# Two transformer layers at decode: all of batch 7's V kept between the layers, a ring of 4 MB for the weights of layer 0, w2 in eight blocks

## The chip, the cores and the metric

The kernel runs on one core of a Trainium2 chip. The metric is the device time of one execution in microseconds (us). A core has engines that run side by side: TensorE (PE in the profile; its weight loads are PEld), VectorE (DVE), ScalarE (ACT), GpSimd (POOL) and SyncE (SP). Here SP does nothing but issue transfers from the chip's main memory. On-chip memory is laid out in 128 partitions.

## The reference

Two equal layers work on eight sequences (batches), one new token each; all is float32, and both layers read the same weights and the same cache.

```
D = 1024; Hq, Hkv, Sk, Dh = 32, 4, 4096, 128; F = 3584; B = 8

def attention(x):                      # x: (8, 1, 1024), x already normed
    q = x @ wq                         # wq 1024 x 4096
    scores = q . k_cache * Dh ** -0.5  # each of 4 K heads serves 8 query heads
    o = softmax(scores) . v_cache
    return o @ wo                      # wo 4096 x 1024

def mlp(x):
    return gelu(x @ w1 + b1) @ w2 + b2 # w1 1024 x 3584, w2 3584 x 1024

for layer in range(2):
    x = x + attention(layernorm(x))
    x = x + mlp(layernorm(x))
```

K and V of one batch are 8.4 MB each, wq and wo 16.8 MB each, w1 and w2 14.7 MB each. The caches are 134 MB for each layer, so the kernel has some 359 MB to read.

## The kernel before

**Memory.** One large tile, `arena`, is cut into 52 units of 1024 columns (`SCW`), 0.52 MB each. Everything that is loaded takes a run of units: a tile of K or V (one of eight for a batch) takes two, and a "piece" of 4 units is 2.1 MB.

**Order of transfers.** A list `stream` is written once, in the order in which the transfers are issued, with the units to which each goes. `pump` issues the first of the list as soon as its units are free, and no other before it. `release` frees units after the last instruction that reads them, and pumps again. All go through SP's queue (the line of `nc.sync.dma_start` in `pump`, L241): an entry whose units are still read by PE holds up all that follow.

**Stages of layer 0.** The queries (`queries`) are made from wq; 28 units of wq (rows `kt` 0 to 6, each in two halves `u`) stay in memory until layer 0 ends, in units 0 to 27, and row 7 is parked elsewhere (`park`, half of it in accumulator memory). The eight batches then run through `attention`: `scores` against K (L545), softmax (`probs`), `values` with V (L588), `heads`. K and V share units 28 to 51. Six of the eight V tiles of the last batch, 7, are not released but stay for layer 1, which runs through the batches from 7 to 0.

**wo, w1.** `project` multiplies with wo (L381), a layernorm follows, and `expand` multiplies with w1 (L270, its last group L273), 512 columns in a group. `hidden_wide` and `hidden_group` turn a group and apply GELU while PE goes on. Both weights pass through units 40 to 51, a ring of 12 units, in pieces of 4 units (two of wo's are 2).

**The swap.** `swap` multiplies with w2 and makes the next layer's queries from the wq that was kept. w2 is cut into four blocks of 256 output columns (`CB`), each with 28 row tiles of 128 (`NFT`). For one block, `down` does 28 products (L418; each float32 product is two matmul records in the profile), DVE copies the sums (L462), PE selects and turns them (L466), DVE adds them to x (L468). With two more rows of x known, PE does the query products of those two rows of wq (`q_part`, L317), and their slots are released. The next parts of w2 and the first K of layer 1 go to those slots. w2, but for its last four row tiles, stays in memory for layer 1; the last four (`LATE`) are read again at the very end.

**Layer 1.** Attention as before, in 28 units; the wo and w1 stages; `down_row` multiplies with the w2 that stayed (L424).

Which part of a block goes to which unit is in this table, by block: (first row tile, number of row tiles, unit).

```
W2_PARTS = (((0, 16, 40), (16, 8, 44), (LAST, 4, 46)), ((0, 4, 47), (4, 16, 48), (20, 4, 46), (LAST, 4, 0)),
            ((LAST, 4, 1), (0, 16, 2), (16, 8, 6)), ((LAST, 4, 0), (0, 16, 8), (16, 8, 12)))
```

Of the kernel before, what the change touches and what calls it, by code (L numbers as in the profile page):

```python
# [38 lines left out]
UNPARK = 14  # L39
# [3 lines left out]
W2_PARTS = (((0, 16, 40), (16, 8, 44), (LAST, 4, 46)), ((0, 4, 47), (4, 16, 48), (20, 4, 46), (LAST, 4, 0)),  # L43
            ((LAST, 4, 1), (0, 16, 2), (16, 8, 6)), ((LAST, 4, 0), (0, 16, 8), (16, 8, 12)))
LATE_AT = 0, 1, 14, 15
# [61 lines left out]
def decode_layers(ctx: ExitStack, tc: tile.TileContext, x, kc, vc, wq, wo, w1, w2, out):  # L107
# [152 lines left out]
    def expand(name, rs, work=None):  # L260
        n = 0
        for slot in tiles((name,)):
            for c in range(0, slot.cols, CH):
                u, kt = divmod(n, NT)
                lhs = xnT[:, kt * XS:kt * XS + 32]
                if kt == 0:
                    acc = ps_o.tile([P, CH], F32, tag="o", name="acc")
                if u < NGR - 1:
                    j = kt % 4
                    nc.tensor.matmul(acc[32 * j:32 * j + 32, :], lhs, slot.ap[:, c:c + CH], start=(kt < 4), stop=(kt >= NT - 4))  # L270
                else:
                    for j in range(4):
                        nc.tensor.matmul(acc[32 * j:32 * j + 32, 0:P], lhs, slot.ap[:, c + j * P:c + (j + 1) * P],  # L273
                                         start=(kt == 0), stop=(kt == NT - 1))
                n += 1
            release(slot)
            if n % NT:
                continue
            if u == 0:
                flush()  # L280
            if u < NGR - 1:
                row = row_s if work or u % 2 else qz[:, P:P + CH]
                nc.scalar.activation(row, acc, AF.Copy, scale=rs)
                if not work:
                    flush()
                pending.append(lambda u=u, row=row: hidden_wide(u, row))
            else:
                if not work:
                    flush()
                row, hid = row_s[:, 0:P], qz[:, P:2 * P]  # L290
                nc.scalar.activation(row, acc[:, 0:P], AF.Copy, scale=rs)
                nc.vector.transpose(hid, row)
                hidden_group(u, lambda pre: nc.vector.tensor_tensor(pre, hid.rearrange("p (t q) -> p t q", t=GT)[:, :, 0:B], bias1(u), ALU.add))
            for f in (work or {}).get(u, ()):
                f()
        assert n == NGR * NT

# [13 lines left out]
    def q_part(acc, u, kt, c0, ap):  # L311

        n = ap.shape[1]
        for j in range(4):
            d0, d1 = max(c0, j * CH), min(c0 + n, (j + 1) * CH)
            if d0 < d1:
                nc.tensor.matmul(acc[u][32 * j:32 * j + 32, d0 - j * CH:d1 - j * CH], xnT[:, kt * XS:kt * XS + 32],  # L317
                                 ap[:, d0 - c0:d1 - c0], start=(kt == 0), stop=(kt == NT - 1 and d1 == (j + 1) * CH))
# [95 lines left out]
    def down(y, c, kts, n0=0):  # L414

        for n, kt in enumerate(kts, n0):
            g = kt % 4
            nc.tensor.matmul(y[32 * g:32 * g + 32], h_at(kt), w2_at[c, kt], start=(n < 4), stop=(n >= NFT - 4))  # L418

    def down_row(y, kts, cs=range(CB)):  # L420

        for kt in kts:
            for c in cs:
                nc.tensor.matmul(y[32 * c:32 * c + 32], h_at(kt), w2_at[c, kt], start=(kt == 0), stop=(kt == NFT - 1))  # L424

    def w2_kts(c, i):

        k0, n, _ = W2_PARTS[c][i]
        return range(k0, k0 + n)

    def arrive(key, kts):
        slot = held[key]
        for e, kt in enumerate(kts):
            w2_at[key[1], kt] = slot.ap[:, e * Q4:(e + 1) * Q4]
        return kts

    def swap():
# [6 lines left out]
        stats = ()  # L444

        def used(kt, u):
            slot = held.pop(("q", kt, u))
            q_part(acc, u, kt, 0, slot.ap)
            release(slot)
            if (kt, u) == (4, 0):  # L450
                st["unparked"] = unpark()

        for c in range(CB):
            y = ys[:, c % 2 * Q4:(c % 2 + 1) * Q4]
            n = 0
            for i in range(len(W2_PARTS[c])):
                kts = arrive(("w2", c, i), w2_kts(c, i))
                down(y, c, kts, n)
                n += len(kts)
            release(held.pop(("w2", c, [k0 for k0, _, _ in W2_PARTS[c]].index(LAST))))  # L460
            ysb = row_s[:, c % 2 * Q4:(c % 2 + 1) * Q4]
# [3 lines left out]
            for i in range(2):  # L465
                nc.tensor.matmul(pt[:, i * B:(i + 1) * B], ysb[:, i * P:(i + 1) * P], bsel, start=True, stop=True)  # L466
            xc = xv[:, 2 * c:2 * c + 2]
            nc.vector.tensor_tensor(xc, pt[:, 0:2 * B].rearrange("p (i b) -> p i b", b=B), xc, ALU.add)  # L468
            if c == CB - 1:
                stats = moments(pt)  # L470
            for kt in (2 * c, 2 * c + 1):
                for u in range(2):
                    if kt < NT - 1:
                        late.append(lambda kt=kt, u=u: used(kt, u))
                        if (kt, u) != (3, 1):
                            late.pop()()
                    elif u == 0:
                        spot = st.pop("unparked")
                        q_part(acc, u, kt, 0, spot.ap)
                        spot.free()  # L480
                    else:
                        slot = held.pop(("qe", 0))
                        q_part(acc, u, kt, 0, slot.ap)
                        q_part(acc, u, kt, W - KEEP, spare)
                        slot.free()
                    if c == CB - 1 and (kt, u) in ((NT - 2, 1), (NT - 1, 0)):
                        next(stats, None)
# [213 lines left out]
    n_kept = 6  # L701
# [24 lines left out]
    for b in orders[0][1:]:  # L726
        batch(0, b, *cycle[(b - 1) % 5])
    weights(("o0",), wo[0], [4, 4, 2, 2, 4, 4, 4, 4, 4], fixed(40, 44, 48, 50, 40, 44, 48, 40, 44))
    weights(("i0",), w1[0], [4] * 7, fixed(48, 40, 44, 48, 40, 44, 48))
    for c in range(CB):  # L730
        for i, (_, _, at) in enumerate(W2_PARTS[c]):
            down_weights(("w2", c, i), c, w2_kts(c, i), at)
    stream.append((("qe", 0), 0, wq[0][:, -W:-KEEP], x_row[:, 0:W - KEEP], ()))
    batch(1, last_b, ((4, 16), (4, 20), (4, 24), (2, 0), (2, 14)), ((4, 16),))
    batch(1, last_b - 1, ((4, 20), (4, 24), (2, 0), (2, 14), (4, 16)), ((8, 28), (8, 16)))
    batch(1, last_b - 2, ((4, 36), (4, 24), (8, 28)), ((8, 16), (8, 24)))
    at = [32, 16, 24] * (4 * B)
    for b in orders[1][3:]:
        batch(1, b, *([(8, at.pop(0)), (8, at.pop(0))] for _ in "kv"))
    weights(("o1",), wo[0], [8, 8, 8, 4, 2, 2], fixed(24, 32, 16, 24, 28, 30))  # L740
    weights(("i1",), w1[0], [4] * 6 + [2, 2], fixed(32, 36, 16, 20, 24, 28, 32, 34))
    for c, e, n in LATE:
        at = (c * NFT + LAST + e) * Q4
# [5 lines left out]
    for layer in range(2):  # L749
# [12 lines left out]
        else:  # L762
# [19 lines left out]
            for c, e, n in LATE:  # L782
                arrive(("late", c, e), range(LAST + e, LAST + e + n))
# [36 lines left out]
def _blocks(w):  # L820
    return w.reshape(NFT, P, CB, Q4).transpose(1, 2, 0, 3).reshape(1, P, -1)
# [38 lines left out]
```

## Time and profile before

| | |
|---|---|
| median of 3 runs | 850.57 us (849.89 to 852.33) |
| the profiled execution | 851.14 us, of which the trace spans 849.4 |
| bytes read | 358.83 MB, 423 GB/s over the span |
| busy | PE 520.2 us (61%), PEld 171.6, DVE 202.2 (24%), ACT 57.0 |
| SP's transfers | 135 issues at L241, all in one queue |
| stages, us from the start | queries to 59; layer 0 attention to 360; wo to 400; w1 to 435; swap to 477; layer 1 attention to 770; wo, w1, w2 to 846 |

A row of a timeline gives the start in us, the duration, the engine, line and operation, what it writes and reads, the shape, how many instructions are taken together, and in brackets how long the engine had been idle and what it waited for. A row of a window gives the stretch and its length, the busy time of PE, PEld, DVE, ACT and POOL with their instruction counts, then the clock that TensorE was granted (1.00 is full), the share of time in which the 16 transfer engines were busy, and GB/s. In the page, DMA and GB/s are given for 40 equal slices of 21.2 us.

### The profile page before, as it was taken

Reading aid. Unit: us, or ns where it says so; the run is one execution under the profiler, and the core shown is the slowest. Engines: PE = TensorE matmul, PEld = TensorE weight load, DVE = VectorE, ACT = ScalarE, POOL = GpSimd, SP = SyncE. Lnnn points to the kernel's source line nnn. Section 1 sums busy time; section 2 is a strip of 40 time slices with the busy share of each in tenths; the row PEclk is TensorE's granted clock in tenths of the full one; section 3 lists DMA queues with packets and bytes.
Section 4 is the critical chain, followed back from the end, with each engine's and each line's share of the span. In section 5 each row is a group of like instructions: output and inputs, shape, how many; then the busy total and the mean of one; then the engine's idle time right before and its main releaser. Section 6 shows DMA issues by size and latency. Waiting matters only on the chain.

```text
span 849.4 us, 9218 instructions
## 1 busy us (share of the span) xinstructions
PE 520.2 (61%) x3962; PEld 171.6 (20%) x3962; DVE 202.2 (24%) x690; ACT 57.0 (7%) x120; POOL 2.2 (0%) x13
## 2 busy tenths in 40 slices
PE   0755755565656647656678775476555566565677
PEld 0211111111111111122133222121111111112333
DVE  0013132222223231400220343231413222231022
ACT  0110000000000000000201100000000000000031
POOL 0000000000000000000000000000000000000000
PEclk9976777786677788877889996868888887869899
DMA  9999999999999999999999999999999999999996
GB/s 401 419 427 436 422 441 419 435 428 432 423 429 441 424 438 418 429 424 427 427 398 416 425 433 426 436 428 433 427 434 428 433 429 432 431 432 430 421 427 273
DMA packets 19768, 359.55 MB, mean 423 GB/s; under 512 B 2192, under 2 KB 2832, under 8 KB 4240
## 3 DMA queue, kind: packets, MB, share of 16 engines
q1 hardware_dynamic: 19584, 358.82, 99.1%
q8 instruction: 31, 0.51, 0.2%
q10 hardware_dynamic: 144, 0.15, 0.1%
q14 instruction: 9, 0.07, 0.0%
HBM read 358.83 MB, written 0.13 MB: 423 GB/s over the span
## 4 chain that ended last, share of the span: by engine, by line
DMA 75%; PE 22%; DVE 1%; issue 1%; another core or an unknown queue 1%; ACT 0%; SPq 0%; ACTq 0%; DVEq 0%
DMA arena<-in_k_dram 29%; DMA arena<-in_v_dram 22%; DMA arena<-in_w_dram 11%; DMA arena<-in_wo_dram 8%; PE sps L545 8%; PE o_ps L588 7%; DMA arena<-in_wq_dram 5%; PE y L381 2%; PE acc L317 1%; PE sps L418 1%; PE acc L270 1%; PE sps L600 0%; ACT sps L569 0%; PE sps L578 0%
## 5 line engine op out<-in xcount | busy, mean ns | idle before, releaser
L545 PE MATMUL sps<-arena,qz 128*32 128x512 f32 x1024 | 162.7, 779 | 118.3 <-DMA arena<-in_k_dram 117.2
L588 PE MATMUL o_ps<-arena 128*32 128x512 f32 x512 | 86.0, 804 | 55.1 <-DMA arena<-in_v_dram 45.9
L588 PE MATMUL o_ps<-arena,spare 128*32 128x512 f32 x512 | 80.8, 748 | 41.2 <-DMA arena<-in_v_dram 34.3
L545 PEld LDWEIGHTS sps<-arena,qz 128*32 128x32 f32 x1024 | 37.2, 133 | 206.3 <-issue 168.6
L593 DVE SCALAR_TENSOR_TENSOR scr<-o_ps,bits,scr 128x128 f32<-128x128 f32 x192 | 67.4, 351 | 6.8
L381 PE MATMUL y<-arena,oxT 128*32 128x256 f32 x512 | 41.8, 484 | 32.8 <-DMA arena<-in_wo_dram 32.8
L591 DVE TENSOR_SCALAR scr<-o_ps,bits 128x128 f32<-128x128 f32 x64 | 22.5, 351 | 145.9 <-PE o_ps L588 145.9
L270 PE MATMUL acc<-arena,oxT 128*32 128x512 f32 x192 | 28.7, 723 | 13.8 <-DMA arena<-in_w_dram 13.3
L600 PEld LDWEIGHTS sps<-bits,scr 128*128 128x128 f32 x128 | 22.1, 217 | 68.3 <-issue 45.7
L317 PE MATMUL acc<-arena,oxT 128*32 128x512 f32 x248 | 32.6, 666 | 5.0 <-DMA arena<-in_wq_dram 3.5
L588 PEld LDWEIGHTS o_ps<-arena 128*32 128x32 f32 x512 | 16.8, 133 | 87.9 <-issue 58.8
L601 DVE TENSOR_TENSOR oxT<-sps,scr 128x8 f32<-128x8 f32 x64 | 10.5, 165 | 93.4 <-PE sps L600 93.4
L550 DVE TENSOR_SCALAR_CACHE_REDUCE spare<-sps 128x512 f32<-128x512 f32 x16 | 11.1, 692 | 87.5 <-PE sps L545 87.5
L588 PEld LDWEIGHTS o_ps<-arena,spare 128*32 128x32 f32 x512 | 16.9, 127 | 69.0 <-issue 48.5
L550 DVE TENSOR_SCALAR_CACHE_REDUCE arena<-sps 128x512 f32<-128x512 f32 x16 | 11.1, 692 | 81.5 <-PE sps L545 81.5
L569 ACT ACTIVATE sps<-arena,bits 128x512 f32<-128x512 f32 x16 | 10.9, 680 | 285.0 <-DVE scr L563 285.0
L381 PEld LDWEIGHTS y<-arena,oxT 128*32 128x32 f32 x512 | 18.9, 134 | 53.7 <-DMA arena<-in_wo_dram 32.7
L569 ACT ACTIVATE sps<-spare,bits 128x512 f32<-128x512 f32 x16 | 10.9, 681 | 268.7 <-DVE scr L563 268.7
L600 PE MATMUL sps<-bits,scr 128*128 128x8 f32 x128 | 28.0, 291 | 0.0
L559 PE MATMUL sps<-scr,bits 128*128 128x128 f32 x32 | 7.6, 322 | 22.9 <-DVE scr L555 22.9
L418 PE MATMUL sps<-arena,oxT 128*32 128x256 f32 x224 | 15.2, 417 | 5.1 <-DMA arena<-in_w_dram 5.1
L201 PE MATMUL sps<-ident,xb 128*128 128x128 f32 x6 | 1.5, 345 | 24.4 <-DMA xb<-in_x_dram 23.3
(125 smaller groups left out, 246.0 us busy)
## 6 DMA issues: line engine op xcount, KB each, us to landing
arena<-in_v_dram SPq DMA_DIRECT2D x26, 4096.0 KB, 21.5
arena<-in_k_dram SPq DMA_DIRECT2D x21, 4096.0 KB, 20.6
arena<-in_k_dram SPq DMA_DIRECT2D x20, 2048.0 KB, 17.6
arena<-in_w_dram SPq DMA_DIRECT2D x17, 2048.0 KB, 12.7
arena<-in_v_dram SPq DMA_DIRECT2D x9, 2048.0 KB, 18.5
arena<-in_wo_dram SPq DMA_DIRECT2D x8, 2048.0 KB, 12.8
arena<-in_wo_dram SPq DMA_DIRECT2D x3, 4096.0 KB, 23.0
arena<-in_w_dram SPq DMA_DIRECT2D x5, 1024.0 KB, 13.5
```

The lines of the kernel that those rows point to most:

```text
L270: nc.tensor.matmul(acc[32 * j:32 * j + 32, :], lhs, slot.ap[:, c:c + CH], start=(kt < 4), stop=(kt >= NT - 4))
L317: nc.tensor.matmul(acc[u][32 * j:32 * j + 32, d0 - j * CH:d1 - j * CH], xnT[:, kt * XS:kt * XS + 32], ap[:, d0 - c0:d1 - c0], start=(kt == ...
L381: nc.tensor.matmul(y[32 * j:32 * j + 32, 0:Q4], lhs[:, n * B:n * B + 32], slot.ap[:, c + j * Q4:c + (j + 1) * Q4], start=(n == 0), stop=(n ...
L418: nc.tensor.matmul(y[32 * g:32 * g + 32], h_at(kt), w2_at[c, kt], start=(n < 4), stop=(n >= NFT - 4))
L545: nc.tensor.matmul(ps[32 * g:32 * g + 32, :], qz[:, c:c + 32], kt[:, g * CH:(g + 1) * CH], start=(j == 0), stop=(j == HKV - 1))
L550: nc.vector.tensor_scalar(st["row", b].ap[:, half * CH:(half + 1) * CH], ps, SCALE, None, op0=ALU.mult, op1=ALU.max, accum_out=st["mx", b] ...
L569: nc.scalar.activation(pp, row[:, h * CH:(h + 1) * CH], AF.Exp, bias=bias, scale=1.0, accum_out=ls[:, h:h + 1])
L588: nc.tensor.matmul(o[32 * g:32 * g + 32, :], s[:, g], v[:, g * CH:(g + 1) * CH], start=(half == 0), stop=(half == NH - 1))
L591: nc.vector.tensor_scalar(r, o[:, 0:P], sel_t[:, 0:1], None, op0=ALU.mult)
L593: nc.vector.scalar_tensor_tensor(r, o[:, t * P:(t + 1) * P], sel_t[:, t:t + 1], r, op0=ALU.mult, op1=ALU.add)
L600: nc.tensor.matmul(po[:, 0:REP], r_s[j % 2], sel_h, start=True, stop=True)
L601: nc.vector.tensor_tensor(oT_v[:, j * REP:(j + 1) * REP, b], po[:, 0:REP], rl_s[b % 2][:, j * REP:(j + 1) * REP], ALU.mult)
```

## The change

All eight V tiles of batch 7 stay in memory (`n_kept` 8). They take units 28 to 43, so the weights of layer 0 pass through units 44 to 51: 8 units, in pieces of 3, 3 and 2. w2 is cut into eight blocks of 128 columns, in the order 1, 0, 2, 3, 4, 5, 6, 7. The first 24 row tiles of a block come in two parts (16 and 8 row tiles: 2 units and 1 unit); the last four row tiles of a pair of blocks come together in one unit. After each block only one row of wq is used, its second half after the products of the next block. Layer 1's ring is 16 to 43, in pieces of the same sizes as before.

```
-UNPARK = 14
+UNPARK = 18
...
+W2_ORDER = ((1, 0), (2, 3), (4, 5), (6, 7))
+W2_PARTS = (((0, 16, 44), (16, 8, 46)), ((0, 16, 48), (16, 8, 50)), ((16, 8, 47), (0, 16, 4)), ((0, 16, 6), (16, 8, 0)),
+            ((16, 8, 1), (0, 16, 2)), ((16, 8, 9), (0, 16, 10)), ((16, 8, 8), (0, 16, 12)), ((0, 16, 14), (16, 8, 51)))
+W2_LAST = 51, 51, 51, 16
...
+LATE_AT = 24, 25, 26, 27
...
-            release(slot)
-            if n % NT:
-                continue
...
+                if c + CH == slot.cols:
+                    release(slot)
+                if n % NT == 0:
+                    hidden(u, acc, rs, work)
...
+    def hidden(u, acc, rs, work):
+        if u == 0 or not work:
+            flush()
+        if u < NGR - 1:
+            row = row_s if work or u % 2 else qz[:, P:P + CH]
+            nc.scalar.activation(row, acc, AF.Copy, scale=rs)
+            pending.append(lambda: hidden_wide(u, row))
...
+            a = w2_at[k, kt]
+            nc.tensor.matmul(y[32 * g:32 * g + 32], h_at(kt), arena.ap[:, a:a + P], start=(n < 4), stop=(n >= NFT - 4))
...
+        for s in range(NT):
+            c, h = divmod(s, 2)
+            k = W2_ORDER[c][h]
+            y = ys[:, s % 4 * P:(s % 4 + 1) * P]
+            n = 0
+            for i, (k0, m, _) in enumerate(W2_PARTS[k]):
...
+                down(y, k, kts, n)
+                n += m
+            if h == 0:
+                arrive_last(("w2", "last", c), c, range(LAST, NFT))
+            down(y, k, range(LAST, NFT), n)
+            if h == 1:
+                release(held.pop(("w2", "last", c)))
+            ysb = row_s[:, s % 4 * P:(s % 4 + 1) * P]
+            nc.vector.tensor_copy(ysb, y)
+            while late:
+                late.pop()()
+            nx = pt[:, s % 2 * B:(s % 2 + 1) * B]
+            nc.tensor.matmul(nx, ysb, bsel, start=True, stop=True)
+            nc.vector.tensor_tensor(xv[:, k], nx, xv[:, k], ALU.add)
+            if k < NT - 1:
+                used(k, 0)
+                late.append(lambda k=k: used(k, 1))
...
-    n_kept = 6
+    n_kept = 8
...
+    batch(0, last_b, ((8, 28), (4, 36), (4, 44)), ((4, 40), (8, 28), (4, 36)))
+    weights(("o0",), wo[0], [3, 3, 2] * 4, fixed(*(44, 47, 50) * 4))
+    weights(("i0",), w1[0], [3, 3, 2] * 3 + [2, 2], fixed(*(44, 47, 50) * 3, 44, 46))
...
+    batch(1, last_b, ((2, 20), (2, 22), (4, 24), (4, 16), (4, 20)), ())
+    batch(1, last_b - 1, ((4, 24), (4, 16), (4, 20), (4, 40)), ((8, 28), (4, 36), (4, 24)))
+    at = [16, 36, 28] * (4 * B)
+    for b in orders[1][2:]:
```

On the host, w2 is laid out in this order of blocks and parts. In `down_row`, a product of 256 columns whose two halves now lie apart is one matmul over both where their distance is a power of two, and otherwise two matmuls of 128 columns.

SP's queue in the swap. Before, from the first transfer of w2 to the rest of wq's row 7 (a row of 1024 columns is one unit):

```order
L241 DMA arena_69<-in_w2_dram 128x4096
L241 DMA arena_69<-in_w2_dram 128x2048
L241 DMA arena_69<-in_w2_dram 128x1024 x2
L241 DMA arena_69<-in_w2_dram 128x4096
L241 DMA arena_69<-in_w2_dram 128x1024 x3
L241 DMA arena_69<-in_w2_dram 128x4096
L241 DMA arena_69<-in_w2_dram 128x2048
L241 DMA arena_69<-in_w2_dram 128x1024
L241 DMA arena_69<-in_w2_dram 128x4096
L241 DMA arena_69<-in_w2_dram 128x2048
L241 DMA xb_79<-in_wq_dram 128x128
```

In the changed kernel, the first twelve rows of the same stretch:

```order
L244 DMA arena_69<-in_w2_dram 128x2048
L244 DMA arena_69<-in_w2_dram 128x1024 x2
L244 DMA arena_69<-in_w2_dram 128x2048
L244 DMA arena_69<-in_w2_dram 128x1024 x2
L244 DMA arena_69<-in_w2_dram 128x2048
L244 DMA arena_69<-in_w2_dram 128x1024
L244 DMA arena_69<-in_w2_dram 128x2048
L244 DMA arena_69<-in_w2_dram 128x1024 x2
L244 DMA arena_69<-in_w2_dram 128x2048
L244 DMA arena_69<-in_w2_dram 128x1024 x2
L244 DMA arena_69<-in_w2_dram 128x2048
L244 DMA arena_69<-in_w2_dram 128x1024
```

Where 13 transfers stood, four of them of 4 units, there are now 20 of 2 units or 1 unit, twelve of them of 1 unit.

PE in the swap. Before, the first two blocks (L418 products, L466 selection, L317 query products of one half row of wq in four matmuls):

```order
L418 MATMUL sps_1529<-arena_69,oxT_81 32x256 x28
L466 MATMUL sps_1531<-bits_75,scr_84 128x8 x2
L317 MATMUL acc_1532<-arena_69,oxT_81 32x512 x4
L317 MATMUL acc_1533<-arena_69,oxT_81 32x512 x4
L317 MATMUL acc_1532<-arena_69,oxT_81 32x512 x4
L317 MATMUL acc_1533<-arena_69,oxT_81 32x512 x4
L418 MATMUL sps_1529<-arena_69,oxT_81 32x256 x28
L466 MATMUL sps_1531<-bits_75,scr_84 128x8 x2
```

In the changed kernel, the first three of eight:

```order
L421 MATMUL sps_1537<-arena_69,oxT_81 32x128 x28
L485 MATMUL sps_1539<-bits_75,scr_84 128x8
L319 MATMUL acc_1540<-arena_69,oxT_81 32x512 x4
L421 MATMUL sps_1537<-arena_69,oxT_81 32x128 x28
L319 MATMUL acc_1541<-arena_69,oxT_81 32x512 x4
L485 MATMUL sps_1539<-bits_75,scr_84 128x8
L319 MATMUL acc_1540<-arena_69,oxT_81 32x512 x4
L421 MATMUL sps_1537<-arena_69,oxT_81 32x128 x28
```

Of each row of wq the second half (acc_1541) has moved behind the next block's products, ahead of that block's selection.

SP's queue at the start of layer 1. Before, from the rest of wq's row 7 on:

```order
L241 DMA xb_79<-in_wq_dram 128x128
L241 DMA arena_69<-in_k_dram 128x4096 x3
L241 DMA arena_69<-in_k_dram 128x2048 x2
L241 DMA arena_69<-in_v_dram 128x4096
L241 DMA arena_69<-in_k_dram 128x4096 x2
L241 DMA arena_69<-in_k_dram 128x2048 x2
L241 DMA arena_69<-in_k_dram 128x4096
L241 DMA arena_69<-in_v_dram 128x8192 x2
```

In the changed kernel:

```order
L244 DMA xb_79<-in_wq_dram 128x128
L244 DMA arena_69<-in_k_dram 128x2048 x2
L244 DMA arena_69<-in_k_dram 128x4096 x7
L244 DMA arena_69<-in_v_dram 128x8192
L244 DMA arena_69<-in_v_dram 128x4096 x2
```

The transfer of V between the two batches' K, two tiles of batch 7, is gone.

148 lines of the change are left out of this document (64 added, 84 removed).

## The prediction

> **What bounds the kernel now.** I read the page's transfer rows first, then the chain of work that ended last, then windows by stage, then the timeline where the change works.
>
> ```profile
> DMA  9999999999999999999999999999999999999996
> GB/s 401 419 427 436 422 441 419 435 428 432 423 429 441 424 438 418 429 424 427 427 398 416 425 433 426 436 428 433 427 434 428 433 429 432 431 432 430 421 427 273
> q1 hardware_dynamic: 19584, 358.82, 99.1%
> HBM read 358.83 MB, written 0.13 MB: 423 GB/s over the span
> DMA 75%; PE 22%; DVE 1%; issue 1%; another core or an unknown queue 1%; ACT 0%; SPq 0%; ACTq 0%; DVEq 0%
> ```
>
> The transfers are busy from the first slice to the last but one, and one queue, SP's, carries 99.1% of them. The chain consists of transfers for 75%. So time is bytes over rate, plus the slices in which the rate falls. Those are the first, the last, and the two near 430 to 465 us (398, 416). By stage:
>
> ```profile
> 340.00:430.00 90.00, 55.09 (x472) 19.65 (x468) 15.94 (x62) 9.90 (x20) 0.00 (x0) 0.78 1.01 427
> 430.00:440.00 10.00, 6.85 (x118) 4.13 (x120) 3.88 (x19) 1.03 (x5) 0.63 (x1) 0.84 1.01 420
> 440.00:450.00 10.00, 8.55 (x110) 3.82 (x100) 1.02 (x3) 0.00 (x0) 0.00 (x0) 0.98 0.96 363
> 450.00:460.00 10.00, 7.20 (x90) 2.65 (x90) 0.60 (x2) 0.00 (x0) 0.00 (x0) 1.00 0.99 415
> 460.00:470.00 10.00, 8.76 (x108) 3.98 (x108) 1.05 (x4) 3.16 (x2) 0.00 (x0) 1.00 1.01 424
> 470.00:480.00 10.00, 8.03 (x70) 3.21 (x66) 4.70 (x18) 2.24 (x4) 0.00 (x0) 1.00 1.00 421
> 490.00:770.00 280.00, 172.18 (x1092) 52.10 (x1092) 82.06 (x265) 12.15 (x32) 0.00 (x0) 0.80 1.00 431
> ```
>
> The last three columns are granted clock, transfer share and GB/s. wo and w1 (340 to 430) run at 427, attention of layer 1 at 431; the stage of w2 with the next layer's queries (the "swap", 430 to 480) averages 409, which against 427 loses 50 x 18 / 427 = 2.1 us, 1.5 of them in 440 to 450.
>
> And a short window inside the first block of w2, with the clock at 0.50:
>
> ```profile
> 437.50:439.50 2.00, 2.00 (x24) 0.84 (x20) 0.00 (x0) 0.00 (x0) 0.00 (x0) 0.50 1.03 426
> ```
>
> **The change, part by part.** (1) Two more tiles of V stay in memory: 2 x 1.05 = 2.10 MB are not read again. At 431 GB/s that is 4.87 us, at 427 4.91; I take -4.9. In this chain a byte left out shortens the end, unless the queue then runs dry. All else is the question whether it does.
>
> (2) The ring for wo and w1 shrinks from twelve units of 0.52 MB to eight, in pieces of 3, 3 and 2 units. The rows:
>
> ```profile
> 396.28 3.44 PE L381 MATMUL y<-arena,oxT 128*32 128x256 f32 x32 [2.33 <-DMA arena<-in_wo_dram]
> 401.41 1.92 PE L270 MATMUL acc<-arena,oxT 128*32 128x512 f32 x16 [0.39 <-DVE oxT L205]
> 421.22 1.92 PE L270 MATMUL acc<-arena,oxT 128*32 128x512 f32 x16 [1.17 <-DMA arena<-in_w_dram]
> 426.12 3.15 PE L270 MATMUL acc<-arena,oxT 128*32 128x512 f32 x16 [2.39 <-DMA arena<-in_w_dram]
> 431.02 1.96 PE L273 MATMUL acc<-arena,oxT 128*32 128x128 f32 x64 [0.74 <-DMA arena<-in_w_dram]
> arena<-in_w_dram SPq DMA_DIRECT2D x17, 2048.0 KB, 12.7
> out_dram<-xb SPq DMA_DIRECT2D x1, 128.0 KB, 1.7
> ```
>
> Four units land every 4.9 us (421.22, 426.12, 431.02): 1.23 us a unit. PE eats four units in 1.92 us at full clock and 3.44 at the lower one. Between issue and first data I allow 1.7 us: that is the whole of the small output transfer, so an upper bound. While PE eats a piece of three, five units (6.1 us) are queued; PE needs 3.44 x 3/4 = 2.6, the issue and its delay 1.7 more. That leaves a spare of 1.8 us at the low clock, 3.0 at the full one. Before, a 2 MB piece took 12.7 us from issue to landing, of which 4.9 its own: a backlog of 7.8. Between wo and w1 PE stops from 396.28 + 3.44 = 399.72 to 401.41, 1.7 us. The pieces behind wo's last hold six units, 7.4 us, so that is covered. Cost 0 by this sum, and not below, since this stage has nothing to win back; upper bound 1.5 us, if all 90 us ran at the 420 of the row 430 to 440 (90 x 7 / 427). I take 0.2, near the sum.
>
> At the end of w1 the pieces are 2 and 2 units, and w2's first piece goes to the place of the former. Behind it only 2 units (2.45 us) are queued, against 32 small matmuls (1.96 / 2 = 0.98) plus 1.7: a gap of 0.2 us.
>
> (3) The swap in eight blocks:
>
> ```profile
> 435.96 4.92 PE L418 MATMUL sps<-arena,oxT 128*32 128x256 f32 x56 [2.41 <-DMA arena<-in_w_dram]
> 440.94 0.33 SPq L241 DMA_DIRECT2D arena<-in_w_dram  x1
> 440.95 0.42 DVE L462 COPY scr<-sps 128x256 f32<-128x256 f32 x1 [4.19 <-PE sps L418]
> 441.52 0.58 PE L466 MATMUL sps<-bits,scr 128*128 128x8 f32 x4 [0.64 <-DVE scr L462]
> 442.14 0.18 DVE L468 TENSOR_TENSOR oxT<-sps,oxT 128x16 f32<-128x16 f32 x1 [0.77 <-PE sps L466]
> 442.37 3.64 PE L317 MATMUL acc<-arena,oxT 128*32 128x512 f32 x32 [0.27 <-DVE oxT L468]
> 445.83 3.20 PE L418 MATMUL sps<-arena,oxT 128*32 128x256 f32 x56
> 455.63 1.93 PE L418 MATMUL sps<-arena,oxT 128*32 128x256 f32 x32 [1.96 <-DMA arena<-in_w_dram]
> ```
>
> PE work in a new block: 56 matmuls of 128 columns at 1.96 / 64 = 0.031 are 1.7 us; one deferred query part, 3.64 / 4 = 0.91, covers DVE's copy; selection 0.58 / 2 = 0.29; DVE's add and its two crossings 0.28; the other query part 0.91. That is 4.1 us, against 3.5 units of transfer, 4.3 us. So at full clock PE keeps up, with 0.2 to spare a block. The sum over eight, 33 us, is what four blocks cost before (3.2 + 3.64 + about 1.4 each). The doubled number of instructions costs nothing as long as the transfers last longer.
>
> Now the releases. Before, the piece issued at 440.94 waited for the whole first block; 56 matmuls took 4.92 us, part of them at the clock of 0.50 shown above, where the next block took 3.20. After, the first block is half as long, but the pieces wait for wq's slots one after the other. From the landing of block 1's last piece: 8 matmuls (0.25), copy (at most 0.42), selection 0.29, add 0.28, query part 0.91 = 2.15, plus 1.7 = 3.85 us until the second piece of block 2 can flow. Queued behind are 2 + 1 + 1 units, 4.9 us: spare 1.0. The shared piece of blocks 2 and 3 waits for the end of block 0: after its last unit lands 24 matmuls (0.75) and 1.7, against three queued units, 3.7: spare 1.2. Then the same pattern repeats with 1 to 3 us. By this the queue never empties. But the row at 440.94 speaks against trusting it: eight units were queued behind the landing at 435.96, to last until 435.96 + 8 x 1.23 = 445.8, so by the same sum its spare was 445.8 - 440.94 - 1.7 = 3.2 us, and yet the rate fell to 363. So a spare under 3 us costs something. Lower bound: the 2.1 us of before disappear (-2.1). Upper bound: 1.5 us at each of five places with a spare under 3 us, 7.5 less the 2.1 of before, +5.4. I take +0.6, near the lower end, since block 1's release no longer waits for a slow long block and 460 to 470 held 424 with a similar mix of pieces.
>
> Twelve pieces of 0.5 MB stand where six stood. The page DMA: Bandwidth & Descriptors of the Trainium skill (Rules for kernel authors) asks for at least 1 MiB in a DMA for full bandwidth. If the swap's 2.1 us were the price of its six small pieces, twelve would lose 4.2: by it the net would be -4.9 + 2.1 = -2.8, a time near 847.8. The 424 GB/s of 460 to 470, with half-MB pieces in it, do not bear it out.
>
> (4) Into layer 1. Keeping all V leaves twelve free units instead of sixteen for the first K.
>
> ```profile
> 466.84 1.07 PE L418 MATMUL sps<-arena,oxT 128*32 128x256 f32 x16 [0.16 <-DMA arena<-in_w_dram]
> 477.17 3.64 PE L545 MATMUL sps<-arena,qz 128*32 128x512 f32 x32 [1.10 <-DVE oxT L501]
> 486.74 1.06 PE L545 MATMUL sps<-arena,qz 128*32 128x512 f32 x8 [1.41 <-DMA arena<-in_k_dram]
> 492.08 3.32 PE L588 MATMUL o_ps<-arena,spare 128*32 128x512 f32 x16 [2.29 <-DVE spare L570]
> 844.89 1.33 PE L424 MATMUL sps<-arena,oxT 128*32 128x256 f32 x12 [0.91 <-DMA arena<-in_w_dram]
> ```
>
> Twelve units last 14.7 us after w2's end. Before, scores started 477.17 - 466.84 = 10.3 us after w2's last landing; one query part of 0.91 now lies ahead of it, so 9.4, and 3.64 / 2 = 1.8 for two tiles and 1.7: 12.9, spare 1.8. After the scores of batch 7 its V needs no transfer; the first freed units come 4.3 us after the last scores (487.8 to 492.08) plus 3.3, while twelve units of batch 6's K are queued. Cost 0, bounds 0 to 1. The rest of layer 1 has the same pieces in renamed places, and the last transfer feeds the same twelve matmuls of 1.33 us. Some w2 matmuls there become two of 128 columns at 0.031 each, the same PE time. GELU's flush now precedes the activation; it lies between transfers, 0.
>
> Sum: -4.9 + 0.2 + 0.2 + 0.6 = -3.9. The profiled execution has 851.14 us (span 849.4), 0.57 above the median of 850.57. 851.14 - 3.9 = 847.2; against the median 846.7.
>
> **The rivals.** A: the gap goes. The finer releases feed the queue all through the swap, its 2.1 us return: 850.57 - 4.9 - 2.1 = 843.6, up to 845. For it: the early half-block release. Against: the spares of 1 us. B: the ring starves the queue. With backlogs of 3 instead of 7 us, the rate of 340 to 480 falls from 421 to about 410, as in the swap: 140 x 11 / 421 = 3.7 us, no measurable change, 849 to 852. For it 363 GB/s at 440 to 450; against, the sum of spares. The page Perfetto Trace Analysis of the Trainium skill (Optimization Strategy) reads repeated bubbles on the engine that should be saturated as too little memory for the next tile; before, the windows show one such dip. C, slower: PE sets the swap's pace. At that half clock a block takes 8.2 us instead of 4.3; each one costs 3.9. It decides from the second such block: two give 850.57 - 4.9 + 7.8 = 853.5, three 857.4. For it: only 0.2 us spare a block; against: a clock of 0.98 to 1.00 from 440 to 480. D: nothing is saved because the two tiles are read in another place; the order shows two pieces of V fewer in layer 1's start, so I give it none.
>
> **Chances.** My case (845 to 848) 0.58, A 0.15, B 0.19, C 0.08. What this measurement can tell from no change is about 0.3%, 2.6 us: 848.0 to 853.1. Faster takes my case and A, 0.73, and a little of B, 0.02; same 0.17; slower 0.08. The range of eight in ten runs from 844.0 (most of A) to 850.0 (half of B); my case's own is 845 to 848.
>
> **What would show it.** 2.10 MB less on q1 (356.7 MB); a window of 430 to 480 near 400 to 415 GB/s; 340 to 430 near 425 with issue to landing of 7 to 9 us instead of 12.7; no wait of scores longer than a piece. I am wrong if the rate of 340 to 430 falls below 415 (B), if PE waits for nothing in the swap while transfers idle (C), or if the swap holds 425 (A).

## The result: slower, 861.17 us for 850.40
The changed kernel takes 861.17 us (median of 6 runs, 856.90 to 866.96), the kernel before 850.40 beside it (849.89 to 852.33). The ratio is 1.0130, with a 95% interval of 1.0083 to 1.0177: slower by 1.3%, 11 us, where 846.7 (844 to 850) was forecast. The profiled execution took 859.55 us (the trace spans 857.7), 8.4 us more than that of before (851.14).

The page after:

```profile
GB/s 397 420 414 432 428 429 433 428 432 429 424 431 430 436 428 425 390 395 381 410 382 372 401 403 417 436 434 429 432 433 424 437 429 429 436 429 429 424 427 278
q1 hardware_dynamic: 21312, 356.72, 98.6%
```

The 2.10 MB are gone (358.82 to 356.72). But nine slices in a row, 17 to 25 (343 to 536 us), lie between 372 and 417 GB/s where before only two of them fell (398, 416). By stage, first after, then before (the last three columns are granted clock, transfer share, GB/s):

```profile
340.00:430.00 90.00, 54.56 (x458) 18.05 (x452) 14.71 (x56) 8.05 (x17) 0.00 (x0) 0.79 0.98 396
430.00:480.00 50.00, 39.51 (x676) 21.60 (x676) 9.04 (x42) 5.48 (x9) 0.63 (x1) 0.97 0.99 383
480.00:530.00 50.00, 33.67 (x240) 10.50 (x239) 18.90 (x66) 5.28 (x12) 0.00 (x0) 0.84 0.99 402
530.00:770.00 240.00, 151.58 (x906) 45.09 (x902) 66.40 (x214) 9.11 (x24) 0.00 (x0) 0.78 1.00 432
```
```profile
430.00:480.00 50.00, 39.39 (x480) 17.79 (x482) 11.26 (x46) 6.43 (x11) 0.63 (x1) 0.96 0.99 409
480.00:530.00 50.00, 33.87 (x250) 11.11 (x242) 16.92 (x54) 3.04 (x8) 0.00 (x0) 0.83 1.01 428
```

Against before: wo and w1 lose 90 x (427 - 396) / 427 = 6.5 us, the swap 50 x (409 - 383) / 427 = 3.0, the start of layer 1 50 x (428 - 402) / 428 = 3.0. With the bytes' -4.9 that is +7.6 of the 8.4; from 530 to 770 nothing is lost (432; before, 431 from 490 on). These are losses by place; the stages themselves end some us later than before (w2's first product starts at 440.2 instead of 436.0). Note the transfer share: it stays at 0.98 to 0.99 while the rate falls by 6 to 10%. Why, the trace doesn't show; what it means is that here the rate has to be read, not the share.

Three places show how. In the ring of wo (the chain of waits, start, duration):

```profile
368.30 8.16 DMA arena<-in_wo_dram
376.50 2.83 PE y L383 x24
379.35 8.29 DMA arena<-in_wo_dram
```

A slot of three units is issued, lands 8.2 us later, is eaten in 2.8 and issued again at once: a turn takes 379.35 - 368.30 = 11.1 us. In a turn the ring moves 8 units, which at full rate take 8 x 1.23 = 9.8. So the ring, not the full rate of the transfers, sets the pace.

Where the ring starts, in windows of 1 us, and SP's row beside it:

```profile
360.00:361.00 1.00, 1.00 (x13) 0.12 (x5) 0.00 (x0) 0.00 (x0) 0.00 (x0) 0.97 0.99 418
361.00:362.00 1.00, 1.00 (x10) 0.49 (x14) 0.87 (x3) 0.00 (x0) 0.00 (x0) 1.00 0.87 369
362.00:363.00 1.00, 1.00 (x12) 0.13 (x4) 0.62 (x3) 0.00 (x0) 0.00 (x0) 1.00 0.61 258
363.00:364.00 1.00, 1.00 (x18) 0.71 (x18) 0.71 (x3) 0.00 (x0) 0.00 (x0) 1.00 0.18 74
364.00:365.00 1.00, 0.90 (x20) 0.26 (x8) 0.77 (x3) 0.00 (x0) 0.00 (x0) 1.00 0.97 176
365.00:366.00 1.00, 0.00 (x0) 0.00 (x0) 0.00 (x0) 0.00 (x0) 0.00 (x0) 1.00 0.81 340
```
```profile
363.21 0.33 SPq L244 DMA_DIRECT2D arena<-in_wo_dram  x1
366.28 0.64 PE L383 MATMUL y<-arena,oxT 128*32 128x256 f32 x8 [1.37 <-DMA arena<-in_wo_dram]
```

The third piece of wo goes to units 50 and 51. Unit 51 holds the last softmax row of batch 7, so the piece is issued only behind the last value product, at 363.21. The queue ran dry before: these six windows lose (6 x 427 - 1635) / 427 = 2.2 us of the 6.5. (The row at 366.28 reads the second piece, the last one issued before the gap; the third is read at 368.84.) Before, this place was the fourth piece, with ten units ahead of it, now there are six. The clock has a part in it: from 358 to 360 the value products ran at 0.50; before, at 358, they ran at 1.00, and the issue came at 359.95.

In the swap (DVE's copy ends a block, L421 are the products):

```profile
443.28 0.29 DVE L481 COPY scr<-sps 128x128 f32<-128x128 f32 x1 [0.74 <-PE sps L421]
445.31 3.19 PE L421 MATMUL sps<-arena,oxT 128*32 128x128 f32 x56
445.40 16.38 SPq L244 DMA_DIRECT2D arena<-in_w_dram  x11
448.55 0.29 DVE L481 COPY scr<-sps 128x128 f32<-128x128 f32 x1 [4.34 <-PE sps L421]
452.58 1.08 PE L421 MATMUL sps<-arena,oxT 128*32 128x128 f32 x32 [0.92 <-DMA arena<-in_w_dram]
...
458.74 0.29 DVE L481 COPY scr<-sps 128x128 f32<-128x128 f32 x1 [3.10 <-PE sps L421]
```

A block takes about 5.1 us ((458.74 - 443.28) / 3) where its transfer needs 4.3, and PE waits for DMA inside it. One block is slow in itself: the products at 445.31 take 3.19 us, since the clock is 0.50 from 446 to 448, and the next pieces wait for its end; the rate in these two windows of 1 us is 258 and 254. At the front of layer 1:

```profile
486.20 5.34 PE L557 MATMUL sps<-arena,qz 128*32 128x512 f32 x32 [0.48 <-DVE oxT L513]
492.48 1.92 PE L557 MATMUL sps<-arena,qz 128*32 128x512 f32 x16 [0.95 <-DMA arena<-in_k_dram]
499.38 3.64 PE L557 MATMUL sps<-arena,qz 128*32 128x512 f32 x16 [4.97 <-DMA arena<-in_k_dram]
```

The last two K tiles of batch 7 (16 of the 64 matmuls) had no room before the scores of the first two were done. They were issued at 489.77 and landed 9.6 us later; PE waited 4.97 us for them.

### The profile page after: what moved, and what is told of

It reads as the page before. It is cut to its first block, busy times and chain, and to the rows that moved or that the text cites. A ratio compares the mean times of both kernels' runs of the same rounds, so it can differ in the third digit from the quotient of the medians.

```text
span 857.7 us, 9758 instructions
## 1 busy us (share of the span) xinstructions
PE 526.4 (61%) x4218; PEld 177.7 (21%) x4218; DVE 203.4 (24%) x698; ACT 56.3 (7%) x120; POOL 2.2 (0%) x13
## 3 DMA queue, kind: packets, MB, share of 16 engines
q1 hardware_dynamic: 21312, 356.72, 98.6%
## 4 chain that ended last, share of the span: by engine, by line
DMA 72%; PE 24%; DVE 2%; issue 1%; another core or an unknown queue 1%; ACT 0%; SPq 0%; ACTq 0%; DVEq 0%
DMA arena<-in_k_dram 26%; DMA arena<-in_v_dram 21%; DMA arena<-in_wo_dram 11%; DMA arena<-in_w_dram 9%; PE sps L557 8%; PE o_ps L600 7%; DMA arena<-in_wq_dram 5%; PE y L383 2%; PE acc L319 1%; PE acc L273 1%; PE sps L421 1%; PE sps L612 1%; PE sps L439 1%; ACT sps L581 0%
## 5 line engine op out<-in xcount | busy, mean ns | idle before, releaser
L557 PE MATMUL sps<-arena,qz 128*32 128x512 f32 x1024 | 167.6, 800 | 117.3 <-DMA arena<-in_k_dram 116.1
L562 DVE TENSOR_SCALAR_CACHE_REDUCE arena<-sps 128x512 f32<-128x512 f32 x16 | 11.1, 692 | 87.6 <-PE sps L557 87.6
L562 DVE TENSOR_SCALAR_CACHE_REDUCE spare<-sps 128x512 f32<-128x512 f32 x16 | 11.1, 692 | 81.4 <-PE sps L557 81.4
L421 PE MATMUL sps<-arena,oxT 128*32 128x128 f32 x448 | 17.4, 293 | 5.4 <-DMA arena<-in_w_dram 5.1
```

Source lines behind the costliest of these rows:

```text
L421: nc.tensor.matmul(y[32 * g:32 * g + 32], h_at(kt), arena.ap[:, a:a + P], start=(n < 4), stop=(n >= NFT - 4))
L557: nc.tensor.matmul(ps[32 * g:32 * g + 32, :], qz[:, c:c + 32], kt[:, g * CH:(g + 1) * CH], start=(j == 0), stop=(j == HKV - 1))
L562: nc.vector.tensor_scalar(st["row", b].ap[:, half * CH:(half + 1) * CH], ps, SCALE, None, op0=ALU.mult, op1=ALU.max, accum_out=st["mx", b] ...
```

## The experiments
Theories: **residence** (a slot is held for PE's time, its own transfer and a delay of several us; where that exceeds the time in which the ring is filled once, the rate falls), with rivals **small or odd pieces** (rows of 12 KB, half-MB transfers, the new order of GELU in `expand`), and **the blocks themselves** or **one entry at the head of the queue** for the swap. Each run stands with its ratio to the kernel before, run on the same chip.

**1. Pieces of 3 in a ring of 12** (kernel before):
```
-    weights(("o0",), wo[0], [4, 4, 2, 2, 4, 4, 4, 4, 4], fixed(40, 44, 48, 50, 40, 44, 48, 40, 44))
-    weights(("i0",), w1[0], [4] * 7, fixed(48, 40, 44, 48, 40, 44, 48))
+    weights(("o0",), wo[0], [3] * 10 + [2], ...)      # 40, 43, 46, 49 in turn
+    weights(("i0",), w1[0], [3] * 9 + [1], ...)
```


> The kernel before with its ring of twelve units for wo and w1, but cut into pieces of 3 units (rows of 12 KB) instead of 4, and with the changed kernel's expand (GELU's flush ahead of the activation, slots released inside a group). Theory ring (the ring of eight units leaves too little queued for 16 transfer engines that do not run level): nothing changes, 850 to 852, 340 to 430 at 425 GB/s. Theory rows (transfers of 12 KB rows, or the new order in expand, run at 385 to 400 GB/s as the trace after shows): some 6 us slower, 856 to 858.

855.08 us, 1.0048 [1.0029, 1.0067].
```profile
370.00:430.00 60.00, 38.61 (x344) 12.79 (x336) 6.43 (x31) 7.33 (x15) 0.00 (x0) 0.86 0.99 417
430.00:440.00 10.00, 2.54 (x68) 2.11 (x68) 3.66 (x19) 1.52 (x5) 0.63 (x1) 0.91 0.66 254
```
```profile
420.96 0.33 SPq L241 DMA_DIRECT2D arena<-in_w_dram  x1
432.95 2.00 SPq L241 DMA_DIRECT2D arena<-in_w_dram  x2
```
By its time this lies between the two theories; the place decides. The loss is one hole at the end of w1: SP stood for 12 us, since w2's first piece (units 40 to 43) waited for w1's last pieces there; 430 to 440 alone loses 10 x (427 - 254) / 427 = 4.1 us. From 360 to 420 the rate is 419 to 430, so pieces of 3 and the order of GELU cost nothing that can be seen.

**2. The ring of 8 units alone** (kernel before, six kept tiles):
```
+    weights(("o0",), wo[0], [3, 3, 2] * 4, fixed(*(44, 47, 50) * 4))
+    weights(("i0",), w1[0], [3, 3, 2] * 3 + [2, 2], fixed(*(44, 47, 50) * 3, 44, 46))
```


> The kernel before, six tiles of V kept and w2 in four blocks, with the changed kernel's ring alone: wo and w1 through units 44 to 51 in pieces of 3, 3 and 2. Theory ring: slower by what 340 to 430 lost in the trace after (396 against 427 GB/s, 6.5 us), 856 to 858. If the loss lies in the swap and in layer 1 only, 850 to 852.

861.33 us, 1.0121 [1.0101, 1.0140].
```profile
360.00:370.00 10.00, 6.00 (x80) 2.40 (x72) 2.34 (x9) 0.00 (x0) 0.00 (x0) 1.00 0.91 343
370.00:430.00 60.00, 37.47 (x300) 12.93 (x300) 4.97 (x24) 6.53 (x13) 0.00 (x0) 0.74 0.95 372
```
The ring alone costs 10 us (0.0121 x 851), more than the 856 to 858 expected, and the hole at 360 to 370 comes with it.

**3. The first K of layer 1 in 12 units alone** (kernel before):
```
-    batch(1, last_b, ((4, 16), (4, 20), (4, 24), (2, 0), (2, 14)), ((4, 16),))
+    batch(1, last_b, ((4, 16), (4, 20), (4, 24), (4, 16)), ((2, 0), (2, 14)))
```


> The kernel before, but the first K of layer 1 gets twelve units instead of sixteen, as in the changed kernel (its fourth piece waits for the scores of the first). If the dips after 480 us (388 and 365 GB/s) come from this, 2 to 3 us slower, 852.5 to 853.5; if they come only from the late scores after the new swap, no change, 850 to 851.

852.49 us, 1.0017 [1.0007, 1.0028].
```profile
480.00:490.00 10.00, 5.03 (x44) 1.08 (x36) 1.42 (x5) 0.00 (x0) 0.00 (x0) 1.00 0.97 390
```
1.4 us (0.6 to 2.4) for twelve units in place of sixteen.

**4, 5, 6. The changed kernel with other pieces in its ring of 8:** four of 2 units, two of 4, eight of 1.
```
-    weights(("o0",), wo[0], [3, 3, 2] * 4, fixed(*(44, 47, 50) * 4))
+    weights(("o0",), wo[0], [2] * 16, fixed(*(44, 46, 48, 50) * 4))    # 4 (w1 likewise)
+    weights(("o0",), wo[0], [4] * 8, fixed(*(44, 48) * 4))             # 5
+    weights(("o0",), wo[0], [1] * 32, ...)                             # 6, units 44 to 51 in turn
```


> The changed kernel with wo and w1 in pieces of 2 units, four of them in the same eight units. Theory ring: PE holds 2 units instead of 3 while it eats, so 1 unit (1.2 us) more is queued; part of the 6.5 us comes back, 3 us, 858 against 861. Theory rows of 12 KB: all of it, 854 to 855. If more transfers cost something each: no gain, 861 or more.

853.68 us, 1.0032 [1.0011, 1.0053]. By its number alone this is what theory rows forecast (854 to 855), not theory ring (858); experiment 1, where rows of 12 KB ran at full rate in twelve units, and experiment 5, which has rows of 16 KB and loses, speak against rows.

> The changed kernel with wo and w1 in two pieces of 4 units in the same eight units. Theory residence: a piece holds its slot for PE's eating, its own transfer and a fixed delay of about 5 us (from the trace after: 11.2 to 11.7 us for a cycle of eight units, less 2.8 of PE and 3.7 of transfer); the ring delivers eight units in that time, at most in 9.8 us. Here 3.6 + 4.9 + 5 = 13.5 us: 311 GB/s from 370 to 430, and some 20 us slower than after, 880. If the delay is the 1.7 us that the prediction allowed, 10.2 us a cycle: 410 GB/s, 862.

864.72 us (two runs), 1.0159 [1.0130, 1.0188]. The rate, 346, lies between the 311 of theory residence and the 410 of the short delay; the 880 us of the former were far too many.

> The changed kernel with wo and w1 in eight pieces of 1 unit (0.5 MB, 60 transfers). Theory residence: 0.9 + 1.2 + 5 = 7.1 us, under 9.8: full rate as with pieces of 2 units (about 420 GB/s), 852 to 854. Theory small pieces (transfers under 1 MB lose rate): 60 x 0.35 us = 20 us more, 873.

854.69 us, 1.0041 [1.0026, 1.0055].

The windows 370 to 430, of 2, 4 and 1 units, then PE's rows of 4 and of 2 units:
```profile
370.00:430.00 60.00, 35.80 (x320) 11.56 (x316) 6.21 (x30) 7.34 (x15) 0.00 (x0) 0.80 1.01 416
```
```profile
370.00:430.00 60.00, 31.43 (x276) 12.29 (x280) 3.73 (x18) 5.73 (x11) 0.00 (x0) 0.74 0.90 346
```
```profile
370.00:430.00 60.00, 49.04 (x316) 11.49 (x316) 6.22 (x30) 7.34 (x15) 0.00 (x0) 0.74 1.02 407
```
```profile
372.64 3.25 PE L383 MATMUL y<-arena,oxT 128*32 128x256 f32 x32 [3.78 <-DMA arena<-in_wo_dram]
378.92 3.52 PE L383 MATMUL y<-arena,oxT 128*32 128x256 f32 x32 [3.04 <-DMA arena<-in_wo_dram]
385.23 3.33 PE L383 MATMUL y<-arena,oxT 128*32 128x256 f32 x32 [2.79 <-DMA arena<-in_wo_dram]
...
arena<-in_wo_dram SPq DMA_DIRECT2D x9, 2048.0 KB, 9.2
```
```profile
380.49 1.93 PE L383 MATMUL y<-arena,oxT 128*32 128x256 f32 x16 [0.56 <-DMA arena<-in_wo_dram]
382.97 1.93 PE L383 MATMUL y<-arena,oxT 128*32 128x256 f32 x16 [0.55 <-DMA arena<-in_wo_dram]
```
Same memory, same bytes: by the medians, cutting the pieces in 2 wins back 7.5 us. Cutting them in 4 costs 3.6 more, which the times alone do not separate from none (the intervals overlap); the rate does, 346 for 398. With pieces of 4 units each slot's turn is 385.23 - 372.64 = 12.6 us, and a piece lands 9.2 us after its issue, of which 4.9 are its own transfer: the delay is 4.3. With pieces of 2 units PE gets one every 2.48 us, which is the transfer's own 2.45. The full rate needs a turn of at most 9.8 us. The account of PE's time at the lower clock + own transfer + 4.3 puts the four cuts on the right side of it:

| units in a piece | PE + own transfer + delay | rate seen, 370 to 430 |
|---|---|---|
| 4 | 3.4 + 4.9 + 4.3 = 12.6 | 346 |
| 3 (with 3 and 2) | 2.8 + 3.7 + 4.3 = 10.8 (11.1 seen) | 398, and 372 in experiment 2 |
| 2 | 1.9 + 2.45 + 4.3 = 8.7 | 416 |
| 1 | 1.0 + 1.23 + 4.3 = 6.5 | 407 |

(The delay is fitted to the first row alone, and is no constant: landings of 3 units in the changed kernel, 8.16, 8.29 and 8.83 us after the issue, give 4.5 to 5.1. The sum is the turn with nothing queued ahead. With pieces of 2 units and of 1 a turn in fact took some 10.1 and 10.3 us, 8 units at 416 and 407, since a piece that goes out in time waits behind others. The rates hold stretches at both clocks.) Eight pieces of half a MB have slack and still run at 407. Against 427 a piece costs 1.23 x 20 / 427 = 0.06 us more; those of 2 units, 1 MiB each, cost 2.45 x 11 / 427 = 0.06 as well. So the prediction's rule of the Trainium skill, at least 1 MiB in a DMA (DMA: Bandwidth & Descriptors, Rules for kernel authors), holds in direction, but at a sixth of the 0.35 us a piece (2.1 / 6) that I had worked out by it.

**7, 8. Eight blocks of w2 alone** (the changed kernel with six kept tiles and the ring of 12 of before): eight units of w2 ahead of wq's slots, and in 8 nominally twelve.
```
-    n_kept = 8
+    n_kept = 6
-W2_PARTS = (((0, 16, 44), (16, 8, 46)), ((0, 16, 48), (16, 8, 50)), ((16, 8, 47), (0, 16, 4)), ...
+W2_PARTS = (((0, 16, 40), (16, 8, 42)), ((0, 16, 44), (16, 8, 46)), ((16, 8, 43), (0, 16, 4)), ...                  # 7
+W2_PARTS = (((0, 16, 40), (16, 8, 42)), ((0, 16, 44), (16, 8, 46)), ((16, 8, 43), (0, 16, 48)), ((0, 16, 50), ...   # 8
```


> w2 in eight blocks alone: six tiles of V kept, twelve-unit ring in pieces of 4, sixteen units for layer 1's first K, but w2 itself still gets only eight units before wq's slots come free. Theory pool (too little can be queued ahead in the swap): 3 us slower than before, 853 to 854, 450 to 470 near 365 GB/s. Theory V (the loss after w1 comes from what V occupies, not from w2's order): 850 to 851.

855.80 us, 1.0054 [1.0037, 1.0070].

> As the run beside it, but w2 gets twelve units ahead: blocks 2 and 3 start in the four units that w1's last piece leaves, and wq's units 4 to 7 go to layer 1's K. Theory pool: the loss goes, 849 to 851. Theory eight blocks (smaller pieces, more waits of PE): as slow as with eight units, 853 to 854.

856.59 us, 1.0061 [1.0043, 1.0079].
```profile
433.44 0.33 SPq L244 DMA_DIRECT2D arena<-in_w_dram  x1
445.17 0.80 SPq L244 DMA_DIRECT2D arena<-in_w_dram  x2
```
In 8 the four more units were hardly used: SP stood from 433.44 to 445.17, because the shared piece of blocks 2 and 3 waits for the end of the second block, and everything behind it waits with it (the 849 to 851 of theory pool did not come). In both, the first block's piece also waited for one of w1's last pieces. So 8 answered nothing on the number of units; 9 mends both.

**9. Eight blocks in the order 0 to 7, twelve units ahead**, the first block in the units that w1 frees first, the shared piece not behind the second block's end:
```
+W2_ORDER = ((0, 1), (2, 3), (4, 5), (6, 7))
+W2_PARTS = (((0, 16, 40), (16, 8, 42)), ((0, 16, 44), (16, 8, 46)), ((16, 8, 47), (0, 16, 48)), ((0, 16, 50), (16, 8, 1)), ...
+W2_LAST = 43, 0, 5, 16
```


> w2 in eight blocks with six tiles of V kept and the twelve-unit ring, as in the two runs before, but with what held their queue taken away: the first block goes to the units that w1 leaves first, the piece shared by blocks 2 and 3 no longer takes the unit of the piece shared by 0 and 1 (SP stood still for it from 433 to 445 us), and all twelve units are in fact used ahead. The blocks run in the order 0 to 7. Theory queue (transfers held behind one entry that waits for its unit): 849 to 851.5. Theory eight blocks (their waits on PE cost in any case): 854 to 857 as before.

851.45 us, 1.0008 [0.9999, 1.0017].

**10. The ring of 8 of experiment 2, with filler matmuls on PE** behind each piece of wo and w1, which keep its clock up and whose products nothing reads:
```
+            fl = small_ps("s")
+            for e in range(6):        # 4 in w1
+                nc.tensor.matmul(fl[...], ident[:, 0:32], spare[:, 0:CH], start=True, stop=True)
```


> The ring of eight units alone (pieces of 3, 3 and 2, six tiles of V, w2 in four blocks; 861.3 in its own run), with filler on PE: after each piece of wo six, and of w1 four, products of 512 columns whose result nobody reads, so that TensorE does not idle and its granted clock may stay up. Theory residence: PE holds a piece of 3 units 1.5 instead of 2.8 us, the cycle of eight units falls from 11.4 to some 10 us: 855 to 857. If the time that PE holds a piece does not matter, or the clock does not rise: 861 or, for the filler's own time, slower.

856.21 us, 1.0059 [1.0041, 1.0077].
```profile
370.00:430.00 60.00, 48.80 (x462) 17.81 (x462) 5.04 (x25) 6.53 (x13) 0.00 (x0) 0.97 0.99 398
```
Three units in wo in experiment 2, and here:
```profile
375.00 2.79 PE L380 MATMUL y<-arena,oxT 128*32 128x256 f32 x24 [1.18 <-DMA arena<-in_wo_dram]
```
```profile
371.68 1.50 PE L384 MATMUL y<-arena,oxT 128*32 128x256 f32 x24 [0.58 <-DMA arena<-in_wo_dram]
```
Late in w1, in experiment 2 and here:
```profile
420.00:430.00 10.00, 7.63 (x40) 1.96 (x40) 2.48 (x12) 1.61 (x4) 0.00 (x0) 0.83 0.89 349
```
```profile
420.00:430.00 10.00, 7.96 (x64) 2.32 (x60) 1.84 (x10) 1.61 (x4) 0.00 (x0) 1.00 0.99 410
```
With more work on PE the kernel is 5.1 us faster than experiment 2, at a clock of 0.97 for 0.74. The gain is not in wo: from 370 to 400 both run at 396. There PE's pieces and the fillers behind them take some 4.0 + 3 x 1.9 = 9.7 us a turn, which by itself is about the transfers' 9.8. It is in w1, from 400 to 430 (348 to 400), and in the hole at the start (343 to 382). In w1 the chain of waits shows a turn of 12.1 us in experiment 2 (400.96 to 413.01), of which PE holds the slot for 3.6, and of 10.4 here (398.76 to 409.15), of which PE holds it for 2.0; the landings are the same, 8.4 and 8.3. That PE's time is part of the turn explains this; no theory of pieces or transfers does.

**11. Seven kept tiles**, a ring of 10 units in pieces of 2, eight blocks in order, fourteen units for the first K:
```
+    n_kept = 7
+    ring = (44, 46, 48, 40, 50) * 6
+    weights(("o0",), wo[0], [2] * 16, fixed(*ring[:16]))
```


> A version built from the findings: seven tiles of V kept (1.05 MB less to read, 2.5 us), ten units for wo and w1 in pieces of 2, w2 in eight blocks in order with no shared unit at the head of the queue, fourteen units for layer 1's first K. By the findings ring 0 to 1, swap -1 to +2, layer 1 +1: 848.5 to 852.

853.38 us, 1.0023 [1.0010, 1.0036]. That missed the 848.5 to 852 expected. The ring holds (420 in 370 to 430), the swap falls to 393, by a hole in 440 to 450 (310).

**12. Experiment 9 with only 8 units ahead** (units 48 to 51 left for K):
```
-W2_PARTS = (..., ((16, 8, 47), (0, 16, 48)), ((0, 16, 50), (16, 8, 1)), ...
+W2_PARTS = (..., ((16, 8, 47), (0, 16, 0)), ((0, 16, 4), (16, 8, 3)), ...
```


> Eight blocks of w2 in the order 0 to 7, six kept tiles of V and the twelve-unit ring for wo and w1 as before, the first block's parts in the units that w1 frees first (as in the kernel with twelve units ahead, which took 851.45). Changed against that one: only 8 units (40 to 47) are filled with w2 ahead of the slots of wq, and units 48 to 51 are left for layer 1's K. Theory pool (eight units ahead are too few in themselves, since each further piece then waits for a half row of wq that is released only after a block's end, and 2 + 1 + 1 units behind it do not cover a delay of 4 to 5 us): 430 to 480 falls to about 380 to 390 GB/s, time 853.5 to 856. Theory head of the queue (the earlier runs with eight units ahead lost only by one entry at the head that waited for a unit which came free late): 430 to 480 at 405 or more, time 851 to 852.

856.48 us, 1.0056 [1.0039, 1.0072]: 0.5 us beyond even the upper end of theory pool, and out of reach of the other. The swap of 9, then of 12, and PE and SP of 12:
```profile
430.00:480.00 50.00, 40.90 (x706) 21.95 (x706) 12.42 (x55) 6.92 (x11) 0.63 (x1) 1.00 1.00 406
```
```profile
430.00:480.00 50.00, 40.04 (x678) 22.79 (x674) 9.46 (x42) 6.33 (x10) 0.63 (x1) 0.92 0.95 365
```
```profile
437.56 0.43 PE L421 MATMUL sps<-arena,oxT 128*32 128x128 f32 x8 [1.12 <-DVE oxT L373]
...
439.05 1.07 PE L319 MATMUL acc<-arena,oxT 128*32 128x512 f32 x8 [0.26 <-DVE oxT L486]
439.93 1.71 PE L421 MATMUL sps<-arena,oxT 128*32 128x128 f32 x56
440.18 0.33 SPq L244 DMA_DIRECT2D arena<-in_w_dram  x1
445.03 1.08 PE L421 MATMUL sps<-arena,oxT 128*32 128x128 f32 x32 [0.45 <-DMA arena<-in_w_dram]
```
The first block can't end before GELU's last group (the wait for DVE at L373), and its query part (439.05 + 1.07) frees the first slot. The next piece goes out at 440.18. By then the second block runs through its 56 products without a wait, so the eight units have landed, and the new one is read at 445.03. With twelve units ahead there is work for this time; with eight there is not. The blocks themselves cost nothing that can be measured (9), the units ahead of them do: (406 - 365) x 50 / 427 = 4.8 us, and the medians differ by 5.0 (by the ratios, 4.1).

## Why the prediction was wrong
The mechanism of the gain was right: 2.10 MB less on the queue, at 2.34 us a MB, and nothing after 530 us eats it up. What failed is that the queue stays full, by one number used in three terms.

**The delay (terms 2 and 3).** I allowed 1.7 us between a slot's release and its data, the duration of one small output transfer, and called it an upper bound. It was neither for this size nor with other pieces under way. The runs show some 4.3 us beyond the own transfer in a ring, and 445.03 - 440.18 - 2.45 = 2.4 with an almost empty queue. Put into the sum of the prediction, 4.3 makes the spare of the ring 1.8 - 2.6 = -0.8 us a turn at the low clock, where 11.1 - 9.8 = 1.3 was seen; at the full clock it leaves +0.4. Term 2 (+0.2, bound 1.5) measured 6.5. The trace of before held the better number: by the prediction's own sum the issue at 440.94 had 3.2 us to spare, and the rate still fell. I noted it, and priced it at 0.6 instead of putting the delay up by 3. (With 4.3 the sum would still leave 0.6 there, so the delay is not the whole of that dip.)

**The row at the ring's start (not in the prediction).** 2.2 of the 6.5 us are the wait for unit 51. The sum counted the ring in its steady turn only, and not what holds its units when it begins.

**The handover (0.2).** I read the table by position; it is by block number, and the first block is 1. Its first piece goes to unit 48, not behind w1's last piece but one. The term priced something that isn't there.

**The swap (+0.6; bounds -2.1 to +5.4).** Measured +3.0, inside the bounds. The spares of 1.0 and 1.2 us become -1.6 and -1.4 with a delay of 4.3, and from 440 to 470 the rate is 364 to 367. Experiments 9 and 12 show that eight units ahead are too few in themselves, in a kernel with the ring of before. The changed kernel also has the shared piece that waits for the second block, as in 7 and 8 (SP issues it at 448.55); but what stands behind it gets its units only at 449.64, so it holds up no more than itself, one unit. PE's pace (rival C) had a part: the block at 445.31 ran at a clock of 0.50, which put off the releases at its end by some 1.2 us (3.19 against 1.95 for the 56 products at 476.38). But it was the only such block, where C needed two; over the stage the clock stood at 0.97, and PE waits for DMA inside the other blocks.

**The first K (0; bounds 0 to 1).** Measured +3.0 over 480 to 530. Twelve units alone cost 1.4 (experiment 3). The rest is the longer wait, 4.97 us at 499.38, after scores that ran at a lower clock (5.34 us for 32 matmuls, before 3.64), and pieces of batch 6 that go to the units of batch 7's kept V: they are issued only behind its value products (510.73 and 515.09), and 510 to 520 falls to 365. This part is read from the trace and was not tried by itself.

**The chances.** Rival B, the ring that starves, is what happened; I gave it 0.19 and a price of 3.7 us over 140 us (to 410 GB/s). The true rates, 396 and 383, cost more than twice as much, which made it slower and not "same". Its sign was lost with its size: a ring that misses its turn loses in every turn.

Added up, the parts alone give +10.3 (ring), +4.6 (eight blocks with eight units ahead, experiment 7) and +1.4 (K), less 4.9: +11.4, against 11.1 by the ratio. That is close, but the parts overlap (in the changed kernel's profile the ring cost 6.5), so it is no proof. The changed kernel also scatters by 10 us, before by 2.4. A ring whose turn fits at the full clock and not at the lower one would do that, but experiment 2, with the same ring, scatters by only 2.5 in four runs; the cause of the scatter stays open. No version tried is faster than the kernel before; the best, experiment 9, saves no bytes.

## What to carry to other kernels
Before giving buffer memory to data that then needn't be read again, work out the turn: consumer's time at its low clock + own transfer + a delay (here 4 to 5 us); it must be shorter than the time in which all slots of the ring are filled once. Where memory is short, cut the pieces finer (pieces of 2 units for 3 gave 7.5 us here). And ask for each transfer at the head of an in-order queue what it waits for, above all at the seams, where the old owner of the first units sets the time.

## What the runs showed of the hardware
**A transfer's end comes late with several under way.** When the queue ran dry at 361 to 364, the rate fell over three windows (369, 258, 74 GB/s; share 0.87, 0.61, 0.18) and not at once, so the 16 engines end at different times, spread over some 3 us. The last piece of that queue was read by PE only at 366.28, over 2 us after the window of 74 GB/s; that the slowest engine sets the landing fits this, but the trace doesn't show what those 2 us are. The Trainium skill says this of the signal: on this kind of queue each engine that a DMA uses counts up a semaphore when its share has landed, and only the full 16 means that all data is there (DMA: Bandwidth & Descriptors, Why a DMA increments its semaphore by 16 and not by 1). The windows fit it, share 0.87, 0.61 and 0.18 before the landing; the signal itself is in no row. How much of the 4.3 us is this unevenness, how much the start, the signal, and pieces still queued ahead, was not separated.

**More work on TensorE made the kernel faster.** Filler matmuls raised the granted clock from 0.74 to 0.97 in 370 to 430, and the time fell from 861.33 to 856.21. The gain is where the slots came free sooner, in w1 (PE holds one for 2.0 instead of 3.6 us).
